# Lightning attention and a tanh-shrink MLP: factor sums started at other products, and P5 of the two-level products in PSUM columns of its own

## The chip, the cores and the metric

The kernel runs on one core of one Trainium2 chip. The metric is the device time in microseconds (us) of one execution. Besides the timed runs there is one profiled execution, from which every view of the trace below comes. Engines are named as the profile names them: PE (matrix multiply), PEld (its weight loads), DVE (vector engine), ACT (scalar engine), POOL (GpSimd, here used to issue DMAs), SP (issues the other DMAs).

## What is computed

The reference, cut to what matters:

```python
# attention: B, H, S, D = 4, 8, 768, 64, causal decay lam per head, blocks of 64 with a running state
intra = (q_blk @ k_blk.T * Dmask) @ v_blk
inter = (q_blk * lam_pow) @ kv_state
out[block] = intra + inter
# bridge: (B, H, S, D) -> (B*S, H*D) = x, 3072 x 512
h = x @ w_in            # w_in 512 x 2048
g = h - tanh(h)
y = g @ w_out           # w_out 2048 x 512
```

All values are 32-bit floats.

## The kernel before, in words

The 3072 tokens are taken in six groups (g = 0 to 5) of 512 tokens: 128 positions of each of the four batches. For a group, `attention` computes x (transposed) into PSUM and SBUF, `up` multiplies it with w_in and applies h - tanh(h), and `down` or `down_twice` multiplies the result with w_out. Group 0 uses plain matmuls (`up_plain`, `down_plain`), and while it runs the weights are loaded, rounded and combined. From group 1 on the two big products are made by a seven-product scheme (Strassen's, in Winograd's form): each 2 x 2 block product needs seven smaller products, n = 1 to 7, of sums of blocks of the left side and sums of blocks of the right side. The sums of blocks of w_out are called factors; they lie in DRAM (`factors`) and are streamed back into SBUF tiles `wb`, of which there is a ring of seven (`RING`), through POOL's DMA queue, in the order that the products need them (`piece`, L581 to L600).

The down products n = 4, 5, 6, 7 and 3 are made with the scheme applied a second time (`down_twice`, L672): each is again seven products P1 to P7, on 128 x 128 quarters, in the order `STEPS` = 1, 2, 6, 5, 7, 3, 4. One such product is four matmuls of 128 columns (u = 0 to 3, L684). P1, P6, P7 and P4 accumulate one on the other in the first 128 columns of one PSUM bank, `y`, and after each of them ACT copies the running sum to a quarter of the output tile `o` (L687). P2 goes to columns 0 to 127 of a second bank, `zw`. Before the change P5 goes to columns 128 to 255 of `zw`, ACT copies it to an SBUF tile `r5` (L687), and P3 is then accumulated on top of it in the same columns. At the end DVE adds `r5` to the last quarter of `o` (L692) and columns 0 to 255 of `zw` to the first two quarters (L693). `down_twice` is called 22 times: three times in group 1, five times in each of groups 2, 3 and 4, four times in group 5.

The two-level products need factors of the second level. Most of them are sums of quarters of `factors`, and they are made on DVE during the up stage of group 1 (for n = 4, 5, 6; numbers t = 0, 1, 2) and of group 2 (t = 3, 4). `load_quarters(t)` (L558) starts four DMAs that bring the four quarters from DRAM (tiles `wq`, which come from the ring of `wb`, or `oq`). `factors_twice(t)` (L572) is a generator of four steps. Each step is one DVE subtraction on 128 x 512 values (L577) and the DMA that writes its result to the DRAM array `fine` (L578, POOL's queue). The four steps are called t1, t2, t3, t4 here: t1 = b12 - b11, t2 = b22 - t1, then b22 - b12 written in place over b12 (t3), and t4 = b21 - t2. t1, t2 and t4 are tiles of the tag `sums`, which has four buffers; the tiles of `inner_weights` (L470) and of `sums_twice` (L664) come from the same four.

The main loop (L801 to L862) calls `up` for the products of each group in the order 2, 6, 5, 7, 1, 4, 3 for u = 0 to 3, where n = 1 stands for the first product of the next u. It counts these products for groups 1 and 2 (`made`, L814), and the table `turns` (L796) says after which product each `factors_twice(t)` begins; from there one step follows each of four successive products. With `(0, 5)` the four steps of t = 0 follow products 5, 6, 7 and 8 of group 1. After the step that ends t = 0, the last loads of quarters, `load_quarters(2)`, are put in the program. After the seventh product of each u in group 1, `inner_weights(u)` adds eight small DVE operations (L477) and two DMAs.

Each engine runs its instructions in the order in which they are queued, and a scheduler that plans the program ahead of time sets this order from a model of durations; the order in the source is its priority. Where `keep_in_program_order` is used, as in `inner_weights`, the source's order is kept. Semaphores are put in by the same planner. In an `up` of group 1, ACT copies products 6 and 1 from PSUM (L448, L443), DVE adds the `w` and `z` banks (L445, L451, L456), ACT applies tanh (L428), and DVE subtracts (L429) and, at n = 3, forms two sums (L459, L460). The bank `z` is begun by product 5 and can be begun again only when L456 has read it; product 3 accumulates on it and can start only when L451 has read it.

Of the kernel before, what the change touches and what calls it, by code (L numbers as in the profile page):

```python
# [9 lines left out]
F32 = mybir.dt.float32  # L10
# [4 lines left out]
AL = mybir.AluOpType  # L15
# [8 lines left out]
def kernel(  # L24
# [32 lines left out]
    nc = tc.nc  # L57
# [8 lines left out]
    NU = DFF // 512  # L66
# [52 lines left out]
    raw, late = {}, {}  # L119
# [164 lines left out]
    def bank(name, tag, bufs):  # L284
        return psum.tile([128, 512], F32, name=name, tag=tag, bufs=bufs)
# [295 lines left out]
    def piece(g, n, x):  # L581

        i = stream.index((g, n, x))
        while sent["n"] < min(i + RING, len(stream)):
            g_, n_, x_ = stream[sent["n"]]
            t = late["pool"].tile([128, 2, 256], F32, name="wb", tag="wb", bufs=RING)
            if isinstance(n_, tuple) and n_[0] == "quarter":
                nc.gpsimd.dma_start(out=t.rearrange("p m (v c) -> p (m v) c", v=2),
                                    in_=quarter_source(n_[1], *divmod(x_, 2)))
            elif isinstance(n_, tuple):  # L590
                nc.gpsimd.dma_start(out=t.rearrange("p m c -> p (m c)"), in_=fine_in[
                    INNER.index(n_[1]), (5, 6, 3).index(x_)].rearrange("p u c -> p (u c)"))
            elif twice(g_, n_):
                nc.gpsimd.dma_start(out=t.rearrange("p m c -> p (m c)"),  # L594
                                    in_=fine[TWICE.index(n_), SUB.index(x_)].rearrange("p u c -> p (u c)"))
            else:
                nc.gpsimd.dma_start(out=t, in_=factors[XAT[FACT[n_][1]]][:, 2 * x_:2 * x_ + 2, :])  # L597
            blks[stream[sent["n"]]] = t
            sent["n"] += 1
        return blks.pop((g, n, x))  # L600

    def store(g, c, t):
        i, j = divmod(c - 11, 10)
        rows = out.rearrange("(b s) d -> s b d", b=B)[ts(g, BLK), 2 * i:2 * i + 2, ts(j, 256)]

        gate = (g, c) == (1, 22)
        op = (nc.sync if gate or g == NG - 1 else nc.gpsimd).dma_start(
            out=rows, in_=t.rearrange("q (m c) -> q m c", m=2))
        if gate:
            tc.keep_in_program_order(op)  # L610

    def otile(name):
        return opool.tile([128, 512], F32, name=name, tag="o")
# [45 lines left out]
    def quarter(g, n):  # L659

        a = hidden(g, HIDAT[FACT[n][0]])
        return tuple(a[:, :, j, ts(i, 128)] for i in range(2) for j in range(2))
# [9 lines left out]
    def down_twice(g, n, zw):  # L672
        a11, a12, a21, a22 = quarter(g, n)
        s1, s2 = low.pop((g, n))
        y = bank("y2", "ya" if n in (4, 6, 3) else "yb", 1)[:, 0:128]
        zw = bank("zw", zw, 1)
        o = res[g, n] = otile(f"q{n}")
        r5 = late["pool"].tile([128, 128], F32, name="r5", tag="r5", bufs=2)
        for x, a, dst, keep in ((1, a11, y, o[:, 0:128]), (2, a12, zw[:, 0:128], None), (6, s2, y, o[:, 128:256]),
                                (5, s1, zw[:, 128:256], r5), (7, a21, y, o[:, 384:512]), (3, a12, zw[:, 128:256], None),  # L680
                                (4, a22, y, o[:, 256:384])):
            wb = piece(g, n, x).rearrange("p m c -> p (m c)")
            for u in range(NU):
                nc.tensor.matmul(out=dst, lhsT=a[:, u, :], rhs=wb[:, ts(u, 128)], start=x in (1, 2) and u == 0,  # L684
                                 stop=u == NU - 1, skip_group_check=True)
            if keep is not None:
                nc.scalar.activation(keep, dst, AF.Copy)  # L687
            if x == 2:
                nc.vector.tensor_tensor(a12, a12, s2, op=AL.subtract)
            if x != STEPS[-1]:  # L690
                yield
        nc.vector.tensor_tensor(o[:, 384:512], o[:, 384:512], r5, op=AL.add)  # L692
        nc.vector.tensor_tensor(o[:, 0:256], o[:, 0:256], zw[:, 0:256], op=AL.add)  # L693
        if n == 6:

            nc.vector.tensor_tensor(o, o, res[g, 1], op=AL.add)
            for x in (4, 5):
                nc.vector.tensor_tensor(res[g, x], res[g, x], o, op=AL.add)
        elif n == 7:
            nc.vector.tensor_tensor(res[g, 4], res[g, 4], o, op=AL.add)  # L700
            store(g, 21, res[g, 4])
            nc.vector.tensor_tensor(o, o, res[g, 5], op=AL.add)
            store(g, 22, o)
        elif n == 3:
            nc.vector.tensor_tensor(o, o, res[g, 5], op=AL.add)
            store(g, 12, o)
        yield
# [85 lines left out]
    late["pool"] = ctx.enter_context(tc.tile_pool(name="late", bufs=1))  # L793


    turns = {1: (0, ((0, 5), (1, 12), (2, 20))), 2: (7 * NU, ((3, 1), (4, 6)))}  # L796
    made, making = [], {}
    load_quarters(0)
    load_quarters(1)
# [1 line left out]
    for g in range(1, NG):  # L801
# [29 lines left out]
        run(p0[2:])  # L831
        sums_twice(g, 5)
        every(down_twice(g, 4, "z"))
        run(p1[0:1])
        sums_once(g, 21, 21, 11)
        sums_twice(g, 6)
        every(down_twice(g, 5, "w"))
        run(p1[1:2])
        if twice(g, 7):
            sums_twice(g, 7)  # L840
        every(down_twice(g, 6, "z"))
        if twice(g, 3):
            sums_twice(g, 3)
# [49 lines left out]
```

## Time and profile before

| what | value |
|---|---|
| three timed runs | 683.32, 684.01, 680.27 us; median 683.32 us |
| profiled execution | 681.97 us |
| its span, first to last instruction | 679.9 us, so 2.1 us lie around it |
| granted clock of PE | 1.0 all through |
| PE busy | 662.5 us (97%) |
| DVE busy | 480.4 us (71%), 878 instructions |
| ACT busy | 201.2 us (30%), 398 instructions |
| POOL busy | 200.9 us (30%) |
| mean DMA rate | 191 GB/s |

The stages can be told by PE's lines: group 0's plain products (L733, L749) fill about 44 to 149 us; group 1's up products (L420) fill about 149 to 215 us with the first down product (L633) at 204.8; its two-level products (L684) begin at 228.2; each of groups 2 to 5 takes about 100 us after that. A line of a timeline reads: start, duration, engine, line, operation, output<-inputs, shapes, count, and in brackets the idle time of the engine just before and what ended it. A matmul's row and its weight load are counted separately, so "x8" is four matmuls and four loads. PE's end times are modelled.

### The profile page before, as it was taken

To read this page: it belongs to the slowest core of one execution; us is meant where nothing else is said; L and a number is where in the kernel's file an instruction comes from. 1 tells how busy PE (TensorE), PEld (TensorE's weight loads), DVE (VectorE), ACT (ScalarE), POOL (GpSimd) and SP (SyncE) were. 2 spreads that over 40 slices of the span, in tenths; PEclk is the share of its full clock that TensorE was granted. 3 is DMA by queue.
4 is the path that set the end of the run, shared out by engine and by line. 5 is a ranking of instruction groups with operands and counts; after the bars stand their busy time and mean duration, and the time that the engine had idled before them with its cause. 6 is when DMAs were issued, how large, how long until landed. Compare 5 with 4: busy or idle time off the path is not lost.

```text
span 679.9 us, 12929 instructions
## 1 busy us (share of the span) xinstructions
PE 662.5 (97%) x4832; PEld 575.9 (85%) x4832; DVE 480.4 (71%) x878; ACT 201.2 (30%) x398; POOL 200.9 (30%) x347
## 2 busy tenths in 40 slices
PE   6899999999799999999999999999999999999998
PEld 5788855558688989988999988899988899988897
DVE  3798858893778963399887358988358977357753
ACT  2664432423231111243112333112333122334120
POOL 0001424216524533223244300244300244400251
PEclk9999999999999999999999999999999999999999
DMA  9869979958867865668598825698831676710394
GB/s 187 219 199 241 284 211 259 301 141 249 243 168 205 253 219 160 150 172 228 139 307 244 232 47 94 156 283 236 244 83 27 151 237 204 230 48 1 111 299 162
DMA packets 163150, 129.59 MB, mean 191 GB/s; under 512 B 133905, under 2 KB 135313, under 8 KB 163089
## 3 DMA queue, kind: packets, MB, share of 16 engines
q0 software_dynamic: 29136, 97.02, 45.2%
q1 hardware_dynamic: 133808, 31.76, 23.6%
q8 instruction: 38, 0.62, 0.4%
q14 instruction: 24, 0.19, 0.1%
q10 hardware_dynamic: 144, 0.00, 0.0%
HBM read 104.34 MB, written 24.38 MB: 189 GB/s over the span
## 4 chain that ended last, share of the span: by engine, by line
PE 66%; issue 14%; DMA 8%; POOL 5%; DVE 5%; ACT 1%; SPq 1%; POOLq 0%; DVEq 0%; ACTq 0%
PE y L420 11%; PE y L684 8%; PE z L420 7%; PE h L733 6%; PE zw L684 6%; PE op L749 5%; PE y L504 4%; POOL wb L594 3%; PE w L633 3%; PE y L633 3%; PE sp L318 3%; PE plain L633 2%; DMA raw<-in_moe_w_in_dram 2%; PE op L369 2%; PE z L504 2%
## 5 line engine op out<-in xcount | busy, mean ns | idle before, releaser
L594 POOL DMA_DIRECT2D wb<-fine x154 | 83.0, 539 | 123.8 <-PE y L684 51.5
L428 ACT ACTIVATE th<-g 128x512 f32<-128x512 f32 x76 | 47.6, 630 | 107.1 <-DVE g L433 32.9
L420 PE MATMUL y<-xt,w 128*128 128x256 f32 x320 | 73.9, 381 | 1.3 <-ACT g L448 1.3
L597 POOL DMA_DIRECT2D wb<-factors x52 | 28.1, 541 | 144.1 <-PE y L633 94.8
L420 PEld LDWEIGHTS y<-xt,w 128*128 128x128 f32 x320 | 59.8, 190 | 10.6 <-ACT g L448 1.7
L429 DVE TENSOR_TENSOR g<-g,th 128x512 f32<-128x512 f32 x76 | 51.9, 688 | 18.9 <-ACT th L428 18.7
L687 ACT ACTIVATE q<-y 128x128 f32<-128x128 f32 x88 | 24.4, 278 | 120.2 <-PE y L684 118.7
L733 PE MATMUL h<-xt,w 128*128 128x256 f32 x256 | 56.2, 381 | 1.0 <-DVE w L275 1.0
L749 PE MATMUL op<-wt,g 128*128 128x512 f32 x128 | 56.5, 595 | 0.0
L733 PEld LDWEIGHTS h<-xt,w 128*128 128x128 f32 x256 | 48.3, 190 | 8.4 <-DVE w L275 1.4
L684 PE MATMUL y<-wb,g 128*128 128x128 f32 x408 | 54.5, 278 | 0.0
L684 PEld LDWEIGHTS y<-wb,g 128*128 128x128 f32 x408 | 49.3, 192 | 1.5 <-issue 0.3
L749 PEld LDWEIGHTS op<-wt,g 128*128 128x128 f32 x128 | 23.8, 190 | 27.7 <-issue 26.5
L420 PE MATMUL z<-tt,ws 128*128 128x256 f32 x160 | 38.2, 382 | 2.5 <-DVE g L456 2.5
L322 DVE TENSOR_TENSOR ss<-sp,mask 128x512 f32<-128x512 f32 x48 | 30.8, 681 | 11.7 <-PE sp L318 11.7
L420 PE MATMUL y<-tt,ws 128*128 128x256 f32 x160 | 37.8, 379 | 0.0
L420 PE MATMUL z<-xt,ws 128*128 128x256 f32 x160 | 37.8, 379 | 0.0
L202 POOL DMA_DIRECT2D raw<-in_moe_w_out_dram x16 | 8.8, 553 | 93.0 <-ACT r L266 60.3
L684 PE MATMUL zw<-wb,g 128*128 128x128 f32 x272 | 36.0, 275 | 0.1
L420 PEld LDWEIGHTS z<-tt,ws 128*128 128x128 f32 x160 | 29.4, 190 | 7.7 <-DVE g L456 3.8
L633 PE MATMUL w<-wb,g 128*128 128x256 f32 x160 | 35.8, 382 | 0.0
L633 PE MATMUL y<-wb,g 128*128 128x256 f32 x160 | 35.3, 379 | 0.0
(169 smaller groups left out, 1295.9 us busy)
## 6 DMA issues: line engine op xcount, KB each, us to landing
wb<-fine POOLq DMA_DIRECT2D x154, 256.0 KB, 4.0
wb<-factors POOLq DMA_DIRECT2D x60, 256.0 KB, 4.1
raw<-in_moe_w_out_dram POOLq DMA_DIRECT2D x16, 512.0 KB, 5.3
v_nat<-in_v_dram SPq DMA_DIRECT2D x24, 256.0 KB, 5.4
factors<-wt POOLq DMA_DIRECT2D x8, 768.0 KB, 5.4
wb<-fine_in POOLq DMA_DIRECT2D x24, 256.0 KB, 4.1
k_nat<-in_k_dram SPq DMA_DIRECT2D x20, 256.0 KB, 5.3
raw<-in_moe_w_in_dram SPq DMA_DIRECT2D x8, 512.0 KB, 6.1
```

Of the source, the lines that this page charges most:

```text
L322: nc.vector.tensor_tensor(ss[:, j], sp[j], mask[:, j], op=AL.mult)
L420: nc.tensor.matmul(out=t[:, m, :], lhsT=wt[:, kt, ts(m, 128)], rhs=x[:, kt, :], start=first and m == 0 and kt == 0, stop=kt == 1, skip_gro ...
L428: nc.scalar.activation(th, src, AF.Tanh)
L429: nc.vector.tensor_tensor(dst(c), src, th, op=AL.subtract)
L504: nc.tensor.matmul(out=dst[:, ts(u, 128)], lhsT=a, rhs=b, start=x in (1, 2, 5) and u == 0, stop=True, skip_group_check=True)
L594: nc.gpsimd.dma_start(out=t.rearrange("p m c -> p (m c)"), in_=fine[TWICE.index(n_), SUB.index(x_)].rearrange("p u c -> p (u c)"))
L597: nc.gpsimd.dma_start(out=t, in_=factors[XAT[FACT[n_][1]]][:, 2 * x_:2 * x_ + 2, :])
L633: nc.tensor.matmul(out=t[:, m, :], lhsT=a[:, u, kt, ts(m, 128)], rhs=wb[:, kt, :], start=first and u == 0 and m == 0 and kt == 0, stop=u = ...
L684: nc.tensor.matmul(out=dst, lhsT=a[:, u, :], rhs=wb[:, ts(u, 128)], start=x in (1, 2) and u == 0, stop=u == NU - 1, skip_group_check=True)
L687: nc.scalar.activation(keep, dst, AF.Copy)
L733: nc.tensor.matmul(out=hm[:, m, :], lhsT=w1[u][:, i, a, ts(m, 128)], rhs=xt[0, t][:, i, :], start=m == 0 and i == 0, stop=i == KI - 1, ski ...
L749: nc.tensor.matmul(out=obank[b], lhsT=g, rhs=wt[:, 2 * a:2 * a + 2, :], start=kt == 0 and a == 0, stop=kt == KH - 1 and a == 1)
```

## The change

Two edits are made. First, the table of group 1 starts the second-level sums after other products: t = 0 after product 7 instead of 5, t = 1 after 14 instead of 12, t = 2 after 21 instead of 20. (The second entry of `turns`, for group 2, is as it was; `load_quarters(2)` follows the last step of t = 0, so it is now placed after product 10 instead of 8.) Second, P5 gets the columns 256 to 383 of `zw` to itself, ACT no longer copies it, the tile `r5` is gone, P3 has columns 128 to 255 to itself, and one DVE operation with a broadcast input adds P5 from the bank to the second and to the last quarter of `o` at once.

```diff
-        r5 = late["pool"].tile([128, 128], F32, name="r5", tag="r5", bufs=2)
         for x, a, dst, keep in ((1, a11, y, o[:, 0:128]), (2, a12, zw[:, 0:128], None), (6, s2, y, o[:, 128:256]),
-                                (5, s1, zw[:, 128:256], r5), (7, a21, y, o[:, 384:512]), (3, a12, zw[:, 128:256], None),
+                                (5, s1, zw[:, 256:384], None), (7, a21, y, o[:, 384:512]), (3, a12, zw[:, 128:256], None),
                                 (4, a22, y, o[:, 256:384])):
...
-        nc.vector.tensor_tensor(o[:, 384:512], o[:, 384:512], r5, op=AL.add)
+
+        o5 = o.rearrange("q (i c) -> q i c", i=2)[:, :, 128:256]
+        nc.vector.tensor_tensor(o5, o5, zw[:, 256:384][:, None, :].to_broadcast([128, 2, 128]), op=AL.add)
         nc.vector.tensor_tensor(o[:, 0:256], o[:, 0:256], zw[:, 0:256], op=AL.add)
...
-    turns = {1: (0, ((0, 5), (1, 12), (2, 20))), 2: (7 * NU, ((3, 1), (4, 6)))}
+    turns = {1: (0, ((0, 7), (1, 14), (2, 21))), 2: (7 * NU, ((3, 1), (4, 6)))}
```

When both programs are planned, the order of PE's instructions and of SP's is the same in both. On POOL only the stretch of group 1's sums differs: the write of t2, t3 and t4 of each turn moves behind one or both of the writes of `inner_weights` (L478), and the loads of `wb` among them move by a few places. On DVE, in group 1, t1 and t2 of t = 0 and t = 1 no longer stand before and after the subtraction of product 4 (L429) and ahead of L456; t1 now stands directly behind L460, t2 among the eight L477, and t3 and t4 behind these and ahead of the next L451. The tiles of tag `sums` are then taken in the order t1, two of `inner_weights`, t2, t4, so that with four buffers t4 is planned to take the buffer of t1 and waits for the DMA that writes t1 to DRAM; before, t4's wait for that DMA is there too for t = 0, with t1 further ahead. On ACT the 22 copies of P5 are gone, and twice the copy of product 1 (L443) changes places with the tanh ahead of it (L428).

## The prediction

> **What bounds the kernel now.** I read the busy shares first, then what PE waited for, then the timelines of PE and DVE around the longest of those waits, then the groups of the lines that the second edit touches.
>
> ```profile
> PE 662.5 (97%) x4832; PEld 575.9 (85%) x4832; DVE 480.4 (71%) x878; ACT 201.2 (30%) x398; POOL 200.9 (30%) x347
> ```
> ```profile
> PE tp L303 <- DMA q_nat<-in_q_dram: 5.1, 1, 5.1
> PE z L420 <- DVE g L456: 2.5, 1, 2.5
> PE sp L318 <- ACT kt L304: 2.4, 3, 1.0
> PE y L420 <- ACT g L448: 1.3, 1, 1.3
> PE h L733 <- DVE w L275: 1.0, 1, 1.0
> PE zw L684 <- DMA wb<-fine: 0.6, 1, 0.6
> ```
>
> PE is busy 97% and idle 17 us. Of its waits the first, third and fifth are in group 0, which the change does not reach. What it can reach is 2.5 + 1.3 = 3.8 us in group 1, and about one more in the two-level products. A gain is capped near 4.5 us, unless matmuls themselves become faster, and they are at their pace: in the chain eight rows of L420 take 1.73 us and eight of L684 0.89 us throughout. The two waits lie together:
>
> ```profile
> 171.09 1.89 PE L420 MATMUL y<-tt,ws 128*128 128x256 f32 x8
> 175.51 1.99 PE L420 MATMUL z<-tt,ws 128*128 128x256 f32 x8 [2.53 <-DVE g L456]
> 178.76 3.72 PE L420 MATMUL y<-xt,w 128*128 128x256 f32 x16 [1.26 <-ACT g L448]
> ```
> ```profile
> 171.30 0.69 DVE L577 TENSOR_TENSOR wt<-wq 128x512 f32<-128x512 f32 x1 [4.22 <-DMA wq<-factors]
> 171.91 0.68 DVE L429 TENSOR_TENSOR g<-y,th 128x512 f32<-128x512 f32 x1
> 174.17 0.69 DVE L577 TENSOR_TENSOR wt<-wq,wt 128x512 f32<-128x512 f32 x1 [1.57 <-DMA wq<-factors]
> 174.78 0.68 DVE L456 TENSOR_TENSOR g<-g,z 128x512 f32<-128x512 f32 x1
> ```
>
> DVE stands 4.22 us in front of t1 and 1.57 us in front of t2, until quarters of the factors have landed. Behind t2 stands L456, which frees bank z. PE had ended product 3 in z at 167.63 + 1.89 = 169.52, so L456 was ready about 5 us before it ran. PE, in need of z at 172.98, waits to 175.51. ACT is held back by the same L456, and L448 is then late for product 7. So 3.8 us of PE come from a DMA landing, through DVE's queue.
>
> **What the Trainium skill says.** "PSUM — Partial Sum Buffer", section "Engine vs sequencer instructions": "ScalarE/VectorE/GpSimdE queues are strict FIFO." The trace agrees: a ready L456 sits 5 us behind a waiting L577. "VectorE: DVE Perf Modes", section on the TRN2 errata, prices a 32-bit tensor_tensor at (N + 151)/0.96 ns: 291, 424 and 691 ns for 128, 256 and 512 columns; the trace has 288, 419 and 688. "DMA: Bandwidth & Descriptors", section "Two DMAs through the same engine are not ordered": data count as landed when the completion semaphore is full; so a buffer that a write reads from is held from issue to landing, 2.4 to 6.1 us for L578 here. The PSUM page's section on bank collisions asks for guards by bank and not by address. In the trace L693 waits for zw products, and I take the new add to wait for P3 too.
>
> **The first edit, part by part.** Times are of the profiled execution.
>
> Removed: both DVE waits. Without them L456 runs at 169.6, and, with the spacing of before (L456 at 186.15, first slot after L460 at 190.11, so 3.96 us), t1 starts at about 173.65. Its quarters landed at 171.3, and t2's, needed near 175.3, at 174.17. Neither waits; the cover on t2 is 1.1 us, and a later landing costs just its excess. z is free at 170.4, PE begins product 5 at 172.98, and L448 ends about 173.6, before product 7 needs it at 174.71. Gain 3.79 us.
>
> Added: four sums in a row ahead of L451, where there were two for t = 0 and t = 1. DVE starts a 512-column sum every 0.60 us and a 128-column one every 0.20. From t1 to t4 there are t1, eight L477, one L429, t2 and t3: 4 x 0.60 + 8 x 0.20 = 4.0 us, so t4 is due at 177.65 and L451, at 178.25, would end at 178.93. PE needs it for product 3 at 179.89 (172.98 + 4 x 1.73). The longer queue alone costs nothing, with 0.9 us to spare.
>
> But t4 takes the buffer of t1 and waits until t1's write has landed. This was so before for t = 0, with t1 and t4 9.7 us apart, so that it never showed. t1 now ends at 174.3, POOL issues 0.3 us later (before: end 171.99, issue 172.29), hence at 174.6, and landing takes L. t4 can run at 174.7 + L, and L451 ends 1.28 us later. PE's stall is L - 3.8. In this stretch L was:
>
> ```profile
> fine<-wt POOLq DMA_DIRECT2D x1, 256.0 KB, 6.1
> fine<-wt POOLq DMA_DIRECT2D x1, 256.0 KB, 4.8
> fine<-wq POOLq DMA_DIRECT2D x1, 256.0 KB, 2.4
> ```
>
> for issues at 172.29, 175.16 and 179.73. The DMA engines' share is 1.01 between 165 and 178 us, and three loads of wq issued from 169.43 on landed only at 175.9 to 177.6. I take 4.5: later than these, earlier than the full wait. Cost 0.7 us, bounds 0 (L = 2.4) and 2.3 (6.1). Behind t4 on DVE stand L451 and the L429s, and for them wait PE and ACT's tanh; on POOL behind t4's write stand three loads of wb, not due before about 201. The same structure returns at t = 1: stall L - 3.8 with an issue near 188. There the last landings were 6.1 and 5.5 beside three loads of wb, then 2.4 and 2.7; those loads now go out some 6 us ahead. I take L = 3.5, so nothing; bounds 0 and 2.3. At t = 2 six DVE steps of the attention (3.6 us: transposes and L308) stand between t2 and t3, so t4 comes later than any landing; one more sum lies ahead of L451, which had 213.40 - 210.58 = 2.8 us to spare. Nothing.
>
> POOL: the fourth wb load goes out after t1 of t = 2, near 201.1, lands 4.2 to 5.2 us later and is needed at about 207.3: hidden, with a microsecond of cover. The last two stand behind t4's write, near 208.8, land at 214 and are needed from 218 on. `fine` for n = 4 is read after 209, long after its writes. The loads of quarters for t = 2 follow t1's write as before. SP's queue is unmoved: its last block for group 2 lands about 231.5 and is needed at 235.
>
> Lost again later: the first two-level products, at 228 before and 225 after, draw a load each 0.89 us with the DMA engines near full, and now more of this lies beside SP's block loads, which end near 233. Two small gaps there, of 0.15 and 0.31 us, show the edge. I take 0.3; bounds 0 and 1.5.
>
> **The second edit.** Removed: 22 ACT copies of 278 ns (6.1 us of ACT) and P3's wait on them. PE shows no wait on `r`: P7's 0.89 us hides the copy. So PE gains nothing. Changed: 22 DVE adds from 288 to about 420 ns, 2.9 us of DVE:
>
> ```profile
> L693 DVE TENSOR_TENSOR q<-q,zw 128x256 f32<-128x256 f32 x22 | 9.2, 419 | 3.8 <-PE zw L684 3.5
> L692 DVE TENSOR_TENSOR q<-q,r 128x128 f32<-128x128 f32 x22 | 6.3, 288 | 18.9 <-ACT q L687 18.5
> L687 ACT ACTIVATE r<-zw 128x128 f32<-128x128 f32 x22 | 6.1, 278 | 12.8 <-PE zw L684 12.8
> ```
>
> DVE waits ahead of L692 in most calls anyway, and L693, next to it, already waits for P3. In groups 2 to 4 one L669 stands behind the new add and is held up to half a microsecond; its reader comes over 4 us later. Only in group 1, near 240, is DVE full: the L689 that P3 waits for ends at 240.09 and P3 starts at 240.19 (the view names ACT there, which had just ended). There 0.13 us of PE is lost. At the end, L723 follows the last matmuls as before. Cost 0.1; bounds -0.3 (the gap at 240) and 0.6 (four groups).
>
> **The sum.** -3.8 + 0.7 + 0 + 0.3 + 0.1 = -2.7 us. On the profiled execution: a span of 679.9 becomes 677.2, with the 2.1 around it 679.3. The profiled 681.97 lies 1.35 below the median of the runs, 683.32; half-way is 682.65, and I put the forecast at 680.0.
>
> **The rivals.** *All is kept*: t1's write lands within 3.8 us; -3.6, 679.0. For it: 2.4 to 3.3 in half of these writes; against: full DMA engines at 172 to 178. *Given back at the two-level products*: the loads of wb lag by 1.5 us more; -1.2, 681.5. For it: landings of 4.3 to 5.4 us there against seven tiles of 0.89; against: groups 2 to 5 run the same pattern with one wait of 0.6. *Slower*: t4 waits on t1's write in both turns and costs 2(L - 3.8); above L = 5.7 this is more than the 3.8 us saved, and at 6.1, with the rest, 4.6 - 3.8 + 0.4 = +1.2, 683.8. For it: 6.1, 6.1 and 5.5 in this stretch; against: these had loads ahead of them that now come earlier or later. To be 0.5% slower needs L above 7; no such write shows it. That the first edit does not remove the wait is excluded by DVE's order: nothing that waits for wq stands ahead of L456.
>
> **The numbers.** Forecast 0.50, all kept 0.20, given back 0.18, slower 0.12. A difference of 0.5% (3.4 us) is about what a measurement of this kernel can tell from no change, and the forecast stands at that line: half of it and nine tenths of "all is kept" are faster by more, 0.43; half of "slower" beyond, for landings not seen here, 0.06; the rest 0.51. The range takes in the cases to 683.2 and, below, 679.0 less 1.5 for the spread of the runs: 677.5.
>
> **What would show it.** Right: PE's waits on L456 and L448 in group 1 gone; L577 no longer waiting for wq; t4 of t = 0 waiting for the write of t1, and PE's product 3 some tenths late; 22 adds near 420 ns; no `r` copies; groups 2 to 5 as long as before. Wrong: a wait in front of L451 over 2 us, waits on wb over 1 us at 225 to 240, or a later group of other length.

## The result, and the profile after

The changed kernel takes 679.0 us (median of 14 runs, 678.04 to 680.67); the kernel before takes 681.79 us in the runs made beside it (14 runs, 679.55 to 684.18). The ratio is 0.9956 with a 95% interval of 0.9942 to 0.9971, so about 3.0 us are gained, 0.44% (2.0 to 4.0 us by the interval; the two medians differ by 2.8). The forecast was 680.0 us, from a change of -2.7 us. The profiled execution took 679.25 us, with a span of 677.5 us at a granted clock of 1.0.

The busy shares and PE's waits after the change:

```profile
PE 662.0 (98%) x4832; PEld 575.5 (85%) x4832; DVE 484.2 (71%) x878; ACT 195.4 (29%) x376; POOL 200.9 (30%) x347
```
```profile
PE tp L303 <- DMA q_nat<-in_q_dram: 5.1, 1, 5.1
PE sp L318 <- ACT kt L304: 2.5, 3, 1.0
PE y L683 <- DMA wb<-fine: 1.8, 4, 0.8
PE zw L683 <- DMA wb<-fine: 1.1, 3, 0.6
PE zw L683 <- DVE s L668: 0.7, 1, 0.7
PE z L420 <- DVE g L451: 0.5, 1, 0.5
```

L456 and L448 are gone from the list (2.5 and 1.3 us before). L451 is new with 0.5 us, and the waits on `wb` in the two-level products, which are L683 now, have grown from 0.8 to 2.9 us. ACT has 22 instructions fewer and DVE has 3.8 us more.

PE's timeline from product 5 of u = 1 to product 3, and DVE's in the same stretch. (A matmul of the kernel shows as two rows of PE, so one product is eight rows, the x8 of PE's lines; its weight loads are PEld's and are not among them.)

```profile
171.34 1.89 PE L420 MATMUL z<-tt,ws 128*128 128x256 f32 x8
173.07 3.62 PE L420 MATMUL y<-xt,w 128*128 128x256 f32 x16
178.93 1.99 PE L420 MATMUL z<-xt,ws 128*128 128x256 f32 x8 [0.52 <-DVE g L451]
```
```profile
168.09 0.69 DVE L456 TENSOR_TENSOR g<-g,z 128x512 f32<-128x512 f32 x1 [0.35 <-PE z L420]
172.29 0.69 DVE L577 TENSOR_TENSOR wt<-wq 128x512 f32<-128x512 f32 x1
174.51 0.68 DVE L577 TENSOR_TENSOR wt<-wq,wt 128x512 f32<-128x512 f32 x1
177.59 0.69 DVE L577 TENSOR_TENSOR wt<-wq,wt 128x512 f32<-128x512 f32 x1 [1.20 <-DMA fine<-wt]
178.20 0.68 DVE L451 TENSOR_TENSOR g<-g,z 128x512 f32<-128x512 f32 x1
```

L456 now runs as soon as PE has ended product 3 in bank z. t1 and t2 have no bracket: their quarters are there. t4, at 177.59, waits 1.20 us for a write `fine<-wt`, which is that of t1, and L451 right behind it is late by as much as PE's 0.52 us show. The write itself was issued at 173.27 and took, from issue to landing, the last number of this line of the DMA view:

```profile
fine<-wt POOLq DMA_DIRECT2D x1, 256.0 KB, 4.3
```

The groups of the second edit. The idle time in front of L693 is not new: before, L692 and L693 had 18.9 + 3.8 = 22.7 us of it, and now the two additions have 17.1:

```profile
L693 DVE TENSOR_TENSOR q<-q,zw 128x256 f32<-128x256 f32 x22 | 9.2, 420 | 16.4 <-PE zw L683 12.0 <-ACT q L686 3.9 <-issue 0.4
L694 DVE TENSOR_TENSOR q<-q,zw 128x256 f32<-128x256 f32 x22 | 9.2, 420 | 0.7
```

To see where the time went I cut PE's work of every profile at the same four matmuls: the first of product 4 of u = 0 in group 1, the first two-level product of group 1, the L318 that follows the first two calls of `down_twice` (n = 4 and 5, fourteen products, called the first pair below), and the first L721 at the end (its line shifts with the edits). The lengths, in us:

| kernel | product 4 starts at | up stage, to the first two-level product | first pair | from there to the end's first matmul |
|---|---|---|---|---|
| before | 165.91 | 62.27 | 13.97 | 427.45 |
| after | 164.44 | 58.72 | 14.89 | 429.20 |
| difference | -1.47 | -3.55 | +0.92 | +1.75 |

These four sum to -2.35 us; the two spans differ by 2.40. The -1.47 lies in group 0, which the change does not reach; the other profiles below start that product at 164.98 to 166.28, and two of them that contain the whole change, `sums5` and `ring8`, at 165.64 and 165.14, so it is chance. The up stage gives 3.55 us. The first pair gives 0.92 back. The 1.75 of the long rest is in part the waits of this one profile: PE's waits on `wb` and on L668 from there to the first L721 sum to 2.2 us, against 1.0 before. How much of it is the change's doing is taken up below.

The bracket of a wait understates what it costs. In the two profiles below in which PE has no wait in the up stage (`sums5` and `t4_inplace_ring8`) this stage takes 57.94 us. Before, it takes that, the 3.79 us of its two brackets, and 0.53 more; after, that, the 0.52 of its one bracket, and 0.26 more. So each wait here cost some 0.26 us beyond its bracket. In the starts of PE's rows one sees how: a row of L420 starts 0.216 us after the one ahead of it, but across the wait of 0.52 us it was 0.898, and then once 0.320, together 0.79 us late.

### The profile page after: what moved, and what is told of

The parts are those of the page before. It is cut to its first block, busy times and chain, and to the rows that moved or that the text cites. A ratio compares the mean times of both kernels' runs of the same rounds, so it can differ in the third digit from the quotient of the medians.

```text
span 677.5 us, 12910 instructions
## 1 busy us (share of the span) xinstructions
PE 662.0 (98%) x4832; PEld 575.5 (85%) x4832; DVE 484.2 (71%) x878; ACT 195.4 (29%) x376; POOL 200.9 (30%) x347
## 4 chain that ended last, share of the span: by engine, by line
PE 71%; issue 13%; DMA 8%; POOL 5%; DVE 2%; ACT 0%; SPq 0%; POOLq 0%; DVEq 0%
PE y L420 11%; PE h L734 8%; PE y L683 8%; PE z L420 7%; PE zw L683 6%; PE op L750 5%; PE y L633 4%; PE y L504 4%; DMA wb<-fine 4%; PE w L633 3%; PE sp L318 3%; POOL wb L594 3%; PE plain L633 2%; PE op L369 2%; PE z L504 2%
## 5 line engine op out<-in xcount | busy, mean ns | idle before, releaser
L428 ACT ACTIVATE th<-g 128x512 f32<-128x512 f32 x76 | 47.6, 630 | 101.3 <-DVE g L433 32.9
L420 PE MATMUL y<-xt,w 128*128 128x256 f32 x320 | 73.8, 380 | 0.0
L420 PEld LDWEIGHTS y<-xt,w 128*128 128x128 f32 x320 | 59.9, 190 | 9.0 <-ACT g L508 0.9
L429 DVE TENSOR_TENSOR g<-g,th 128x512 f32<-128x512 f32 x76 | 51.9, 688 | 18.9 <-ACT th L428 18.7
L683 PE MATMUL y<-wb,g 128*128 128x128 f32 x408 | 54.4, 278 | 0.0
L683 PEld LDWEIGHTS y<-wb,g 128*128 128x128 f32 x408 | 49.3, 192 | 1.2 <-issue 0.3
L420 PE MATMUL z<-xt,ws 128*128 128x256 f32 x160 | 37.9, 380 | 0.5 <-DVE g L451 0.5
L420 PE MATMUL z<-tt,ws 128*128 128x256 f32 x160 | 38.1, 381 | 0.0
L420 PE MATMUL y<-tt,ws 128*128 128x256 f32 x160 | 37.8, 379 | 0.0
L683 PE MATMUL zw<-wb,g 128*128 128x128 f32 x272 | 36.1, 276 | 0.2 <-DMA wb<-fine 0.2
L420 PEld LDWEIGHTS z<-xt,ws 128*128 128x128 f32 x160 | 30.3, 190 | 5.0 <-DVE g L451 0.9
```

The lines of the kernel that those rows point to most:

```text
L420: nc.tensor.matmul(out=t[:, m, :], lhsT=wt[:, kt, ts(m, 128)], rhs=x[:, kt, :], start=first and m == 0 and kt == 0, stop=kt == 1, skip_gro ...
L428: nc.scalar.activation(th, src, AF.Tanh)
L429: nc.vector.tensor_tensor(dst(c), src, th, op=AL.subtract)
```

## The experiments

The first theory is that of the prediction: two DVE waits are removed from the front of L456, a shorter one on the landing of t1's write comes, and a little is given back where the two-level products draw on the ring. The first rival is that the P5 edit brings the gain or a good part of it; the second, that moving t = 1 and t = 2 matters too.

**The two edits apart.** `turns_only` has only the new table, with P5 and `r5` as before. `p5_only` has only the P5 edit.

```diff
-    turns = {1: (0, ((0, 5), (1, 12), (2, 20))), 2: (7 * NU, ((3, 1), (4, 6)))}
+    turns = {1: (0, ((0, 7), (1, 14), (2, 21))), 2: (7 * NU, ((3, 1), (4, 6)))}
```

> Only the table of start steps is changed (7, 14, 21); P5 is copied to r5 as before. Theory (the gain is the wait of DVE for the quarters' landing ahead of L456): the whole change's gain, ratio 0.9956 within 0.001, PE's waits on L456 and L448 in group 1 gone, t4 of t = 0 waiting about a microsecond for t1's write. Rival (the gain, or a good part of it, comes from P5 in its own columns): ratio 0.998 or above. Second rival (the new add with its broadcast costs time in the later groups): faster than the whole change by 0.5 us or more, ratio 0.9949 or below.

> Only P5's columns and the add from the bank are changed; the start steps are 5, 12, 20 as before. Theory: ratio 1.000 within 0.001, since P7 hides the copy and DVE waits ahead of the add anyway; PE's waits on L456 and L448 as before (2.5 and 1.3 us). Rival (P5's copy was on the path): 0.998 or below. Second rival (the wider add delays the a12 sum and the transposes): 1.001 or above, with PE waits on DVE or later transposes in groups 1 to 4.

`turns_only`: 679.78 us (5 runs), ratio 0.9949 [0.993, 0.9968]. `p5_only`: 682.13 us (14 runs), ratio 0.9996 [0.9982, 1.0009]. The gain is the table's. The P5 edit is worth nothing that these runs can tell from zero: by the interval of `p5_only` it lies between 1.2 us gained and 0.6 us lost. The second rival of `turns_only`, that the new addition costs half a microsecond, is not excluded by the ratio, which lies on its line of 0.9949 with an interval that takes in both. In `p5_only` PE's wait on L456 is still there:

```profile
PE z L420 <- DVE g L456: 2.0, 1, 2.0
PE zw L683 <- DVE gS L688: 1.0, 1, 1.0
```

Its second line is the place in this profile where PE waits for P5's addition: in the second call of the first pair, P3 waits for L688, and L688 stands behind the first call's additions on DVE. The pair took 14.24 us, 0.27 more than before. DVE's timeline of `p5_only` shows why it is more than the 0.13 us by which the new addition is longer:

```profile
234.33 0.41 DVE L693 TENSOR_TENSOR q<-q,zw 128x256 f32<-128x256 f32 x1
234.78 0.42 DVE L694 TENSOR_TENSOR q<-q,zw 128x256 f32<-128x256 f32 x1
235.15 0.71 DVE L298 STREAM_TRANSPOSE qt<-q_blk 128x512 f32<-128x512 f32 x1
```

L694 begins 0.45 us after L693, and L298 0.37 after that, 0.82 in all. In the kernel before, L692, L693 and L298 begin at 235.29, 235.50 and 235.83, 0.54 in all. The two additions now share a quarter of `o`: the second reads what the first has written and starts only after its end, where the two of before overlapped by 0.07 us. In the three calls of this profile in which L669, which does not read that quarter, comes next behind L693, it starts 0.34 us after it; L694 next behind it starts 0.45 to 0.46 after in all 19.

**Only t = 0.** `t0_only` is the kernel before with t = 0 alone moved:

```diff
-    turns = {1: (0, ((0, 5), (1, 12), (2, 20))), 2: (7 * NU, ((3, 1), (4, 6)))}
+    turns = {1: (0, ((0, 7), (1, 12), (2, 20))), 2: (7 * NU, ((3, 1), (4, 6)))}
```

> Start steps 7, 12, 20: only t = 0 is moved, P5 as before. Theory: all of the gain lies in t = 0, so as turns_only, ratio 0.9956 within 0.001; t = 1 and t = 2 have their quarters long before. Rival (moving t = 1 and t = 2 also frees something on PE): half of the gain or less, 0.998.

679.75 us (6 runs), ratio 0.9949 [0.9931, 0.9966], no different from `turns_only`, and the up stage takes 58.75 us against 58.65. The moves of t = 1 and t = 2 give and cost nothing that can be seen here.

**The place of t1.** If the wait for the landing is what costs, then the cost follows the instruction behind which the wait stands, and not the number of sums or their traffic. `t0_at_6` begins t = 0 after product 6, `t0_at_3` after product 3; all else is as before.

```diff
-    turns = {1: (0, ((0, 5), (1, 12), (2, 20))), 2: (7 * NU, ((3, 1), (4, 6)))}
+    turns = {1: (0, ((0, 6), (1, 12), (2, 20))), 2: (7 * NU, ((3, 1), (4, 6)))}
```

> Start steps 6, 12, 20: t1 of t = 0 stands ahead of L456 as before, t2 behind L460. Theory (what costs is L456 standing behind a waiting sum, and its last one decides): DVE still waits about 4 us ahead of t1, but L456 then ends near 172.6 in the times of before, ahead of the 172.98 at which PE wants bank z, so that wait is gone; L448 ends near 175.7 where product 7 is due at 174.7, so about 1 us stays. Gain 2.8 of 3.8 us less 0 to 0.5: ratio 0.9965 within 0.001. Rival (the 4.2 us wait ahead of t1 is the one that PE pays for): ratio 0.999 or above, with PE waiting over 2 us.

> The kernel before with start steps 3, 12, 20: t = 0 begins two products earlier than in the kernel before. Theory (each instruction behind a waiting sum on DVE pays for the landing): t1 now stands ahead of L451 and waits about 10 us, to 171.3 in the times of before; L451 ends at 172.6, where product 3 wanted bank z at 167.6, so PE waits 5.0 us there, and about 0.8 us on L448 later: 5.8 us against 3.8 before, 2 us slower than before, ratio 1.003 within 0.0015. Rival (an earlier start of the sums gets them out of the way): faster than before.

`t0_at_6`: 679.83 us (15 runs), ratio 0.9962 [0.9949, 0.9974]. Here t1 still stands ahead of L456 and t2 no longer does. DVE, then PE:

```profile
171.25 0.69 DVE L577 TENSOR_TENSOR wt<-wq 128x512 f32<-128x512 f32 x1 [2.31 <-DMA wq<-factors]
171.86 0.68 DVE L456 TENSOR_TENSOR g<-g,z 128x512 f32<-128x512 f32 x1
```
```profile
172.59 1.99 PE L420 MATMUL z<-tt,ws 128*128 128x256 f32 x8
175.84 3.72 PE L420 MATMUL y<-xt,w 128*128 128x256 f32 x16 [1.25 <-ACT g L448]
```

The wait before product 5 is gone, since L456 runs at 171.86 against 174.78, 2.6 us earlier when both are counted from product 4. L448 is still 1.25 us late. So the two waits of PE come apart: t2's wait held back bank z, and t1's alone is enough to hold back ACT's chain to L448.

`t0_at_3`: 684.96 us (9 runs), ratio 1.0031 [1.001, 1.0052], slower than before. Its lines on DVE and on PE:

```profile
170.38 0.69 DVE L577 TENSOR_TENSOR wt<-wq 128x512 f32<-128x512 f32 x1 [9.97 <-DMA wq<-factors]
170.99 0.68 DVE L451 TENSOR_TENSOR g<-g,z 128x512 f32<-128x512 f32 x1
```
```profile
171.73 3.66 PE L420 MATMUL z<-xt,ws 128*128 128x256 f32 x8 [4.86 <-DVE g L451]
```

The quarters of t1 land near 170.4 to 171.3 in the three kernels in which it waits for them. The earlier t1 is placed, the more of DVE's work stands behind it: product 3 of u = 0 waits 4.86 us. With 3, 5, 6 and 7 in the table, the up stage takes 64.73, 62.27, 59.62 and 58.75 us. The ratio of `t0_at_3` came out as expected in part by luck: the 0.8 us on L448 did not come, and 1.7 us of slowed matmuls, of which the last section tells, took its place.

**The buffer of t1.** The prediction's one new wait, t4 for the write of t1, should vanish if the tag `sums` gets a fifth buffer. `sums5` is the changed kernel with that number at all four places of the tag, as here:

```diff
-        t1, t2, t4 = (late["pool"].tile([128, NU, 128], F32, name=f"wt{x}", tag="sums", bufs=4) for x in (1, 2, 4))
+        t1, t2, t4 = (late["pool"].tile([128, NU, 128], F32, name=f"wt{x}", tag="sums", bufs=5) for x in (1, 2, 4))
```

> The changed kernel with five buffers of the tag of the sums instead of four, so that t4 of t = 0 no longer takes t1's buffer and no longer waits for t1's write. Theory: DVE's idle time ahead of t4 (1.2 us in the changed kernel's profile) is gone, PE's wait of 0.5 us on L451 is gone, nothing else moves: 0.5 us, which the ratio cannot show (0.9950 within 0.0015) but the profile can. Rival (L451 is late because four sums stand ahead of it, not because of the buffer): PE still waits on L451 0.3 us or more.

```profile
177.52 0.68 DVE L577 TENSOR_TENSOR wt<-wq,wt 128x512 f32<-128x512 f32 x1
```

The wait went: t4 has no bracket, L451 ran at 178.12, and PE had no wait on L451. The up stage took 57.94 us, 0.78 less than after: the 0.52 of the bracket and the 0.26 beside it. But the kernel takes 678.84 us (22 runs), ratio 0.9951 [0.9939, 0.9964], no different from the changed kernel: its first pair takes 15.74 us, the longest of all, where nothing else had been expected to move. In this profile what is gained in the up stage is lost again at once.

**The ring.** So the two-level products have a limit of their own: a load of `wb` goes out when one of seven tiles comes free. `ring8` is the changed kernel with an eighth; `t4_inplace_ring8` also removes t4's wait, by writing t4 over b21 instead of into a fifth buffer; `ring8_before` is the kernel before with the eighth tile alone.

```diff
-    RING = 7
+    RING = 8
```
```diff
-        t1, t2, t4 = (late["pool"].tile([128, NU, 128], F32, name=f"wt{x}", tag="sums", bufs=4) for x in (1, 2, 4))
-        for x, dst, a, b in ((5, t1, b12, b11), (6, t2, b22, t1), (7, b12, b22, b12), (4, t4, b21, t2)):
+        t1, t2 = (late["pool"].tile([128, NU, 128], F32, name=f"wt{x}", tag="sums", bufs=4) for x in (1, 2))
+        for x, dst, a, b in ((5, t1, b12, b11), (6, t2, b22, t1), (7, b12, b22, b12), (4, b21, b21, t2)):
```

> The changed kernel with eight tiles wb instead of seven. What PE gained in group 1's up stage (about 4 us in four profiles) shrinks to about 2 by the end, in waits on wb in the two-level products. Theory (the loads' latency is longer than the lead of the ring, the rate suffices): one tile more is 0.89 us more of lead, PE's waits on wb (2.9 us in the changed kernel's profile) fall below 1 us, ratio 0.993 within 0.0015. Rival (the DMA engines' rate is the limit in these stretches): waits on wb stay above 2 us, ratio as the changed kernel's, 0.9956.

> The changed kernel with eight tiles wb, and t4 written in place over b21, so that it needs no tile of the sums. Both theories together: no PE wait on L451 in group 1 and PE's waits on wb below 1 us; ratio 0.992 within 0.0015. Rival (rate and queue length are the limits): 0.9950 or above.

> The kernel before with eight tiles wb instead of seven and nothing else. In the profiles of before and of the P5 edit alone PE waits 0.8 to 1.0 us on wb, in the five with t = 0 moved 2.1 to 3.8 us. Theory (the waits on wb grow because PE comes to the two-level products earlier, so that part of the gain is given back there): here the eighth tile can save about 0.8 us, ratio 0.9988 within 0.0015, against 2 us in the changed kernel. Rival (the waits on wb are much the same in both and the profile of before was a lucky one): about 2 us here too, ratio 0.997 or below.

`ring8`: 677.06 us (6 runs), ratio 0.9927 [0.9909, 0.9944]. `t4_inplace_ring8`: 676.59 us (6 runs), ratio 0.9919 [0.99, 0.9938], the lowest median measured here, though its interval is not apart from that of `ring8`. The waits on `wb` fall from 2.9 us to 0.7 and 0.2. `ring8_before`: 679.87 us (22 runs), ratio 0.9967 [0.9956, 0.9978]. Here my theory fell and the rival was right on the time: I had put the waits on `wb` down to the change, and the eighth tile saves some 2.2 us (1.5 to 3.0) in the kernel before as well. The profile of before lists only 0.8 us of such waits in the two-level products and 0.3 at L721. But from the first pair's end on it takes 1.67 us longer than `ring8_before` (427.45 and 425.78), 0.9 of it in brackets, and the rest is about what three more waits cost beside their brackets. With t = 0 moved and seven tiles, five profiles list more waits on `wb` than the three with it in place (2.1 to 3.8 us against 0.8 to 1.0). The runs do not show it: the eighth tile saves about 2.0 us with the change and 2.2 without. So the change does not bring these waits about, and how much it adds to them is open.

**The block loads beside it.** In the kernel before, SP's block loads for group 2 are issued until about 229.2 us and the first pair begins at 228.2; after, until 227.7 against 223.2. The stage has moved forward by 5 us and SP by under 2, so that 4.5 us of the two now lie together instead of 1.1. `sp_early` is the changed kernel with these loads cut short: for the last two of the four batches, q and k of group 2 come by one transfer each instead of sixteen. With it SP's last block load is issued at 202.7.

```diff
+                if g == GB and b > 1:
+                    tc.keep_in_program_order(nc.sync.dma_start(
+                        out=x.rearrange("s p r (a c) -> s (p r a) c", c=32).rearrange("s (h e) c -> s h (e c)", e=2),
+                        in_=src[b, :, ts(g, BLK), :].rearrange("h s d -> s h d")))
+                    raw[g, b][name + "b"] = x
+                    continue
```

> The changed kernel, with the q and k blocks of group 2's batches 2 and 3 each loaded by one transfer in natural order instead of sixteen block transfers, so that SP's stream of loads ends some 25 us earlier, before group 1's two-level stage. It leaves out the block-wise transposition of these loads, so part of the attention is computed from untransposed blocks. Theory A (the wb loads land late in group 1's two-level stage because SP's block loads run beside them): that stage, from its first L683 matmul to the next L318, falls from 14.9 us to 14.0-14.3, TensorE's waits on wb between 220 and 240 us vanish, and the kernel is 0.5-1 us faster than the changed one (ratio to before 0.994-0.995). Rival B (the lead of the ring of 7 is shorter than the landing of its own loads, whoever else loads): the stage stays at 14.6-14.9 us with waits on wb of 0.5 us and more, and the ratio stays at 0.9956.

677.6 us (4 runs), ratio 0.9921 [0.9893, 0.9949]. The pair took 14.21 us, as the theory had it, and between 220 and 240 us PE has no wait on `wb`. Twelve loads of `wb` were issued from 224 to 238 us and landed after a median of 3.6 us; of the twelve from 222 to 236 us in the changed kernel it was 5.5, and of those from 227 to 241 us in the kernel before 4.3. After, the last stretch of this pair, and `sp_early`, whose lines are numbered six higher:

```profile
234.33 1.13 PE L683 MATMUL y<-wb,gS 128*128 128x128 f32 x8 [0.76 <-DMA wb<-fine]
236.10 1.13 PE L683 MATMUL zw<-wb,gS 128*128 128x128 f32 x8 [0.64 <-DMA wb<-fine]
```
```profile
234.87 1.06 PE L689 MATMUL y<-wb,gS 128*128 128x128 f32 x8
236.85 1.16 PE L689 MATMUL zw<-wb,gS 128*128 128x128 f32 x8 [0.92 <-DVE gS L694]
```

With the loads out of the way P3 waits for DVE instead. That is the floor which the P5 edit has raised: 13.97, 13.97 and 13.96 us in `before`, `t0_at_3` and `ring8_before`, 14.24, 14.21 and 14.08 in `p5_only`, `sp_early` and `t4_inplace_ring8`. In the changed kernel the loads of `wb` account for all of the 0.92 us given back in this pair: `turns_only`, without P5's additions, also takes 14.89, by one wait of 1.63 us on `wb` ahead of P7, after which P3 does not wait at all. Without SP's block loads 0.68 of it comes back (14.89 to 14.21), and P5's floor keeps the other 0.24. One profile does not fit: `t0_only` takes 14.56 with no wait over 0.2 us on `wb`; there P3 waits 0.92 us for DVE, and why longer than before is open. The run of `sp_early` also shifts other loads between 192 and 229 us, and the median's fall of 0.3% against the changed kernel (intervals overlapping) is more than this one pair's 0.7 us; the rest of it is not explained. The profile's own time doesn't show the fall, because PE was 1.4 us later at product 4 (165.85 against 164.44), before any load that the edit touches.

## Why the prediction was right, step by step

**The two waits removed (-3.8).** Right. Counted from product 4 of u = 0, L456 was forecast at 3.69 us and ran at 3.65; t1 at 7.74, ran at 7.85. (The forecast start of t1 was 173.65; its own working, 169.6 + 3.96, gives 173.56.) The two waits were worth more than their brackets, 4.33 us with the 0.26 that goes with each. The 1.1 us of cover on t2 held: no L577 waited for `wq`. `t0_at_6` and `t0_at_3` show the mechanism, since the cost moves with what stands behind the wait. "PSUM — Partial Sum Buffer", section "Engine vs sequencer instructions", in the Trainium skill states the strict order of DVE's queue; in `t0_at_3` an L451 that follows the waiting t1 stood behind it for 10 us.

**t4 behind the write of t1 (+0.7).** Right in place, close in size. The landing took 4.3 us where I had taken 4.5, and PE's wait was 0.52, 0.78 with what goes with it. `sums5` took it away by a buffer, which shows the cause. At t = 1 the write took 2.4 us and nobody waited (I had taken 3.5); at t = 2 nothing, as forecast. The forecast of -3.8 + 0.7 = -3.1 for the up stage stands against -4.33 + 0.78 = -3.55, and -3.62, -3.52 and -2.65 in `turns_only`, `t0_only` and `t0_at_6`.

**Given back at the two-level products (+0.3).** The mechanism was right, "more of this lies beside SP's block loads", as `sp_early` shows. The size was too small: 0.92 us in the first pair, 0.68 of which ends with SP's block loads. The bound of 1.5 held it, but a sign of being wrong that the prediction named did come: waits on `wb` over 1 us at 225 to 240, here 0.76 + 0.64 = 1.40. What I had left out of this term is that the seven tiles cost time in the kernel before too, some 2.2 us by `ring8_before`.

The prediction's other such sign, a later group of other length, stays open. From the first pair's end on, the three ring-7 profiles with t = 0 left in place take 427.5 to 428.4 us (before, `p5_only`, `t0_at_3`), the six with it moved 428.4 to 429.2, and the ring-8 ones 425.8 to 427.1. The runs leave less room: their -3.0 us, less -3.55 and +0.92, leaves -0.4 for everything else (-1.3 to +0.7 by the interval), an estimate that takes the two stages to be as in these profiles.

**The sum.** That -2.7 comes so near to the measured -3.0 is in part luck. The up stage gained 0.45 us more than forecast: 0.27 because a wait costs more than its bracket, 0.18 because t1's write landed sooner. The first pair gave back 0.92 us where 0.3 and P5's 0.1 were forecast. The two misses nearly cancel.

**P5 (+0.1).** Right to within what can be measured. The additions take 420 ns, where "VectorE: DVE Perf Modes" in the Trainium skill prices them at 424 in its section on the TRN2 errata, and P3's lost wait was worth nothing that shows. In the first pair, where DVE is full, the cost was 0.27 us in `p5_only` instead of 0.13: I had compared durations, and the dependence between the two additions also takes their overlap away. In the changed kernel even this was hidden behind the loads of `wb`.

**The rivals.** "All is kept" was wrong in its working, as t1's write took 4.3 us and not 3.8, and that the time came out at its 679.0 is luck: the runs beside the changed kernel put before at 681.79 and not at the 682.65 from which I started. "Given back" had 1.5 us of lag; 0.92 came in the first pair, and how much later is open. "Slower" needed a landing above 5.7 us in both turns; it was 4.3 and 2.4. (The 6.1 us that the prediction took as the longest holds for group 1; one write of L578 in group 2 of the same profile took 7.0.) The order on SP held, and so did `fine`'s cover on POOL.

## What to carry to other kernels

An instruction that waits for a transfer to land charges its wait to all that stands behind it on its engine (10 us of DVE in `t0_at_3`), so a side task belongs behind the last instruction that the bottleneck engine is due to need, even if that makes the side task later. Then look at what its tiles rotate through, since a task drawn closer together can meet its own writes, as t4 did. And before working on a stage, ask what the next stage waits for: here 0.8 us more gained upstream in `sums5` did not show in the time, while an eighth tile in the ring gave 2 us with and without the change. Whether the 0.8 us count once the tile is there, 676.59 against 677.06 us does not tell.

## What the hardware showed that I had not expected

A wait of PE can cost more than its bracket, and not only by the 0.26 us of the up stage. In `t0_at_3`, after the 4.86 us of idle time, the same eight rows took 3.66 us instead of 1.89. The stretches of that profile (time, sum, busy time of PE, PEld, DVE, ACT and POOL with counts, granted PE clock, DMA share, GB/s):

```profile
171.00:173.00 2.00, 1.27 (x3) 1.09 (x4) 1.30 (x4) 1.29 (x3) 1.63 (x3) 0.68 1.13 257
173.00:175.00 2.00, 2.00 (x6) 1.55 (x6) 2.00 (x5) 0.31 (x1) 2.00 (x4) 0.50 1.05 273
175.00:177.00 2.00, 2.00 (x11) 1.77 (x10) 1.24 (x3) 0.63 (x1) 1.48 (x4) 0.97 0.97 276
```

The granted clock is at half for 3.41 us (171.72 to 175.13) and then full again. "TensorE: Matmul & The Clock Gate" in the Trainium skill, section "The HAM clock gate", tells of this: the clock is halved after an idle window of about 3.4 us, and the windows run freely. The halving and its length agree. But no whole window had to be idle: in `p5_only` a wait of 2.03 us was followed by 3.41 us at half, in `ring8_before` one of 2.67 us likewise, while in the kernel before a wait of 2.53 us left the clock full.

The windows explain this, and the clock record of each trace gives their place. The stretches at full clock ahead of the three halvings last 160.43, 160.43 and 163.84 us, which is 47, 47 and 48 times 3.413; the one of the kernel before, from 13.86 us on, lasts 665.6, which is 195 times. Counted off in such steps, the wait of `p5_only` (172.19 to 174.22) lies within the window from 171.36 to 174.77, that of `ring8_before` (172.26 to 174.92) within the one from 171.89 to 175.30, and at the end of these windows the clock falls. The wait of the kernel before (172.98 to 175.51) is divided by the end of a window at 174.29 into 1.31 and 1.22 us, and with the beginning of the wait for L448 no window there has more than 1.42. So 2.03 us of idle time in one window were enough, and 1.42 were not. Between them the profiles give no sharp limit: in `sp_early` the clock fell at 24.66 us after a window with 1.51 us idle, and in `turns_only`, near the end, one with 1.69 left it full. PE's ends are modelled, so these idle times are estimates.

A halving cost the up stage 1.7 to 1.9 us, which is what is left of its length without the 57.94, the brackets and the 0.26 for each wait. In `p5_only` and `ring8_before` it took the place of the wait for L448, and the stage was little longer or shorter for it (62.10 and 62.64 us against 62.27).

The runs show how often this happens, since each has its mean clock on record; by the figures above one halving in 680 us lowers the mean by 0.0025. A mean of 0.998 or less stands at 41 of the 95 runs of the kernel before that were made beside the experiments, at all 9 of `t0_at_3`, and at 6 of the 59 runs of the six kernels in which PE waits for neither L456 nor L448 (after, `turns_only`, `t0_only`, `sums5`, `ring8`, `t4_inplace_ring8`). The mean does not tell where in the run the halving lay. In the kernel before, the 24 runs at 0.997 have a median of 682.19 us and the 54 above them 682.16, but the 17 at 0.995 or less 683.96. So the gain is not the clock's: at full clock it is 678.95 us after (13 runs) against 682.16. That the removed waits also remove most of the halvings is a small gain on top, which the prediction did not count.
